# Loading q and k alike for both row groups, and the first stage's k and v in runs of tokens

## Chip, core and metric

The program runs on one core of one Trainium2 chip. The time is in device microseconds (us), and a kernel's figure is the median of its runs.

## What is computed

The input has 4 batches of 8 heads, 576 tokens and 64 numbers per head, all in fp32. The first half is attention with a rotary embedding, the second half a gated feed-forward block with a convolution over three tokens. The reference, cut to its core:

```python
def rotate(x):                      # x1, x2: the two halves of the 64 numbers of a token
    return concatenate([x1 * cos - x2 * sin, x1 * sin + x2 * cos])
scores = matmul(rotate(q), rotate(k).T) / sqrt(64)
attn = exp(scores - max(scores)) / sum
x = matmul(attn, v)                 # heads side by side: 4 x 576 x 512
h = maximum(x @ w_in, 0)            # 512 -> 1024
conv_out = sum of h[t - 1], h[t], h[t + 1], each times its row of conv_w
out = (h * sigmoid(conv_out)) @ w_out
```

## The kernel before, in words

**Pairs and steps.** Two heads make a pair, so there are 16 pairs, numbered p. A pair takes five steps (STEPS at L35): four blocks of 128 queries for each head, and a fifth with the last 64 queries of both. Pair p's first step is n = 5p. Nothing is left to a scheduler: `at(n, rank, fn)` (L695) puts a piece of work into step n, each step is written out in the order of its ranks, and each engine takes its instructions in that order. The DMA queue of SP is such an order too: an instruction of SP that has to wait holds up every later load on SP.

**Two stages.** Steps 0 to 25 (WIDE is 26, L681) are the first stage. In it the attention of pairs 0 to 4 runs beside the conversion of the fp64 weights to fp32 and to a high and a low part. From step 26 on, the matmuls of the feed-forward block fill the gaps of the attention.

**q and k.** A pair's q (or k) is loaded (`load`, L142 to L151) into a tile of 128 partitions. Each head has 64 of them, in two row groups of 32. Partition i of a group holds the 18 tokens 32c + i. The first group holds each token as it is (L149: one DMA of runs of 256 bytes), the second with its two halves exchanged (L150 and L151: two DMAs of runs of 128 bytes). So a part takes six DMAs. `rope` (L186) multiplies the tile on POOL with a table of the same layout, `tabt` (L190, six instructions), and adds the two halves (L193, three). That leaves x1 cos - x2 sin in the first group and x1 sin + x2 cos in the second. `emit_TQ` (L230) then transposes blocks of 32 x 32 on DVE into qT (L234) or kT (L237, all 18 blocks in one instruction); the last two k blocks go into the small tile kr as well (L241). The tiles rq and rk have one buffer each, so the next load waits for the transpose of the pair before. Pair 0 is loaded and rotated in another way (`load0`, `rope0`).

**Scores and softmax.** L261 and L287 make the scores of a block on PE, L269 its negated row maximum on DVE, L273 the exponentials on ACT, L321 and L352 turn them on PE, L199 copies them to `pt` on ACT.

**v.** `load_v` (L155) brings a pair's v at step n + 1: per head 512 tokens into the tile vm (L161, partition i holds the tokens i, 128 + i, ...) and the last 64 into vr (L162), four DMAs in all. `emit_E` (L383, the matmuls at L389) multiplies from step n + 5 on; head 0 and head 1 take turns over the four pieces of vm, and vr comes last.

**The sums.** `emit_rinv` (L363) takes the reciprocals of the row sums at step n + 5, writes them to DRAM in four small DMAs (L371) and reads them back spread over the partitions in three (L374 to L376, the tile rb). The norm (L403) multiplies with rb on DVE, at steps n + 8 and n + 9 in the first stage. Its high part is made on ACT (L406), the low part on POOL (L410).

**When loads are issued.** In the first stage q of pair p is loaded at step n - 9 and k at step n - 7, both with rank 19; the rope stands at step n - 6 with rank 18; the transposes of q stand at step n - 4, those of k at n - 2, with rank 0.45 (L723 to L726).

Of the kernel before, what the change touches and what calls it, by code (L numbers as in the profile page):

```python
# [20 lines left out]
def attention_moe_kernel(ctx, tc, q, k, v, w_in, conv_w, w_out, tab, tabx, out):  # L21
# [97 lines left out]

    raw = {}  # L120
    rot = {}

    def load0():
        r = raw[0] = {}
        for nm in ("q", "k"):
            r[nm] = wkeep.tile([128, 4, 2, D], F32, name="r" + nm)
        r["r"] = wkeep.tile([128, 2, D], F32, name="rr")

        def main(nm, src, eng):
            for h in range(2):  # L130
                eng.dma_start(out=r[nm][:, :, h, :], in_=src[0, h, 0:512, :].rearrange("(t p) d -> p t d", p=128))

        nc.sync.dma_start(out=tabs[:, 0:256], in_=tab[:, 0:256])
        main("q", q, nc.scalar)
        nc.sync.dma_start(out=tabs[:, 256:512], in_=tab[:, 256:512])
        main("k", k, nc.sync)
        nc.scalar.dma_start(out=tabs[:, 512:640], in_=tab[:, 512:640])
        nc.scalar.dma_start(out=idf, in_=tab[:, 640:768])
        nc.sync.dma_start(out=r["r"][0:64], in_=q[0, 0:2, 512:S, :].rearrange("h p d -> p h d"))
        nc.sync.dma_start(out=r["r"][64:128], in_=k[0, 0:2, 512:S, :].rearrange("h p d -> p h d"))  # L140

    def load(p, part):  # L142
        b, hp = divmod(p, NPB)
        x = raw[p, part] = p1.tile([128, S // 32, 2, 32], F32, tag="r" + part, name="r" + part)
        for h in range(2):
            y = (q if part == "q" else k)[b, 2 * hp + h].rearrange("(c i) d -> i c d", i=32)
            r0 = slice(64 * h, 64 * h + 32)
            r1 = slice(64 * h + 32, 64 * h + 64)
            nc.sync.dma_start(out=x[r0].rearrange("i c e d -> i c (e d)"), in_=y)  # L149
            nc.sync.dma_start(out=x[r1, :, 0, :], in_=y[:, :, 32:64])  # L150
            nc.sync.dma_start(out=x[r1, :, 1, :], in_=y[:, :, 0:32])  # L151

    vmain = {}

    def load_v(p):  # L155
        if p < 2:
            nc.vector.memset(vrem[p], 0.0)
        b, hp = divmod(p, NPB)
        t = vmain[p] = p1.tile([128, 2, 4, D], F32, tag="vm", name="vm", bufs=2)
        for h in range(2):  # L160
            nc.sync.dma_start(out=t[:, h], in_=v[b, 2 * hp + h, 0:512, :].rearrange("(t p) d -> p t d", p=128))  # L161
            nc.sync.dma_start(out=vrem[p % 2][64 * h:64 * h + 64, h, :], in_=v[b, 2 * hp + h, 512:S, :])  # L162

    def rope0(part, eng):
        x = raw[0][part]
# [19 lines left out]

    def rope(p, part):  # L186
        x = raw[p, part]
        for a in range(0, 18, 3):
            y = x[:, a:a + 3]
            nc.gpsimd.tensor_tensor(out=y, in0=y, in1=tabt[:, a:a + 3], op=ALU.mult)  # L190
        for a in range(0, 18, 6):
            y = x[:, a:a + 6]
            nc.gpsimd.tensor_tensor(out=y[:, :, 0, :], in0=y[:, :, 0, :], in1=y[:, :, 1, :], op=ALU.add)  # L193
# [36 lines left out]
    def emit_TQ(p, part):  # L230
        qk_tiles(p)
        x = raw.pop((p, part))[:, :, 0, :]
        if part == "q":
            nc.vector.transpose(out=QT[p].rearrange("p (c i) -> p c i", i=32), in_=x)  # L234
        else:
            kt = KT[p].rearrange("p (c i) -> p c i", i=32)
            nc.vector.transpose(out=kt[:, 2:20], in_=x)  # L237
            if p * STEPS < WIDE:
                for h in range(2):
                    r = slice(64 * h, 64 * h + 64)  # L240
                    nc.vector.transpose(out=krem[p % 2][r, r].rearrange("p (c i) -> p c i", i=32), in_=x[r, 16:18])  # L241
            if p * STEPS + STEPS > WIDE:
                nc.vector.transpose(out=kt[:, 0:2], in_=x[:, 16:18])
# [115 lines left out]
            at(late["n"], 5 if late["n"] > WIDE else 11, lambda dst=dst[:, i], ps=ps: evac("A", dst, ps))  # L359

    rb = {}

    def emit_rinv(p):  # L363
        rv = rvc[p % 2]
        rt = p1.tile([128, 32], F32, tag="rt", name="rt")
        nc.vector.tensor_scalar(out=rv[:, 0:9], in0=sums[p], scalar1=1e-9, scalar2=None, op0=ALU.add)
        nc.vector.reciprocal(out=rv[:, 0:9], in_=rv[:, 0:9])
        nc.vector.transpose(out=rt, in_=rv)
        d = scr.tile([9, 128], F32, tag="d", name="rd")
        for i in range(0, 128, 32):  # L370
            nc.sync.dma_start(out=d[:, i:i + 32], in_=rt[i:i + 9, :])  # L371
        fl = d.rearrange("(o t) n -> o (t n)", o=1)
        rbt = rb[p] = p1.tile([128, S], F32, tag="rb", name="rb")
        nc.sync.dma_start(out=rbt[0:64, :], in_=fl[:, 0:S].to_broadcast([64, S]))  # L374
        nc.sync.dma_start(out=rbt[64:128, 0:512], in_=fl[:, 640:1152].to_broadcast([64, 512]))
        nc.sync.dma_start(out=rbt[64:128, 512:S], in_=fl[:, 576:640].to_broadcast([64, 64]))  # L376
# [321 lines left out]
    def emit():  # L698
        with tc.manual_schedule(engines=engines):
# [5 lines left out]
            rope0("r", nc.vector)  # L705
            for part in "qrk":
                emit_TQ0(part)
            nc.sync.dma_start(out=tabt, in_=tabx.rearrange("p (c e d) -> p c e d", e=2, d=32))
            load(1, "q")
            load_w(0)  # L710
            emit_S(0, 0)
            load(1, "k")
            load_w(1)
            load_v(0)
# [3 lines left out]
            for p in range(1, NP):  # L718
                n = STEPS * p
                early = n - 10 >= WIDE - 1  # L720
                for i, part in enumerate("qk"):
                    if p > 1:
                        at(max(n - 10, WIDE) if early else n - 9 + 2 * i, 19.6 if early else 19, lambda p=p, part=part: load(p, part))  # L723
                    at(n - 8 + i if early else max(n - 6, 0), 18, lambda p=p, part=part: rope(p, part))
                    at(n - 5 + i * (n - 15 < WIDE) if early else max(n - 4 + 2 * i, 2), 0.45, lambda p=p, part=part: emit_TQ(p, part))
                at(n + 1, 19, lambda p=p: load_v(p))  # L726
            for p in range(NP):
# [19 lines left out]
                else:  # L747
                    for i in range(2):
                        m = n + 5 + (i if n + 5 < WIDE else 0)
                        at(m, 4 if m < WIDE else 10, lambda p=p, i=i: emit_E(p, i))  # L750
                at(n + 5, 4.5, lambda p=p: emit_rinv(p))
                for j in range(2):
                    at(n + NORM.get(p, 8 if n + 8 < WIDE else 7) + (j if p <= WIDE // STEPS else 0), 1.7 + j, lambda p=p, j=j: norms.pop((p, j))())
            whole, done = sum(c for c, _ in wsteps), 0
# [68 lines left out]
def _tables(S, D):  # L823
# [6 lines left out]
    for f in (np.cos(fr), np.sin(fr)):  # L830
# [5 lines left out]
    parts = [res[0], res[2], res[1], res[3], np.eye(128, dtype=np.float32)]  # L836
    root = float(D) ** -0.25
    cs = [(root * np.cos(fr)).astype(np.float32), (root * np.sin(fr)).astype(np.float32)]
    cs = [x.reshape(S // 32, 32, half).transpose(1, 0, 2) for x in cs]
    turned = [np.stack([cs[0], x], axis=2) for x in (-cs[1], cs[1])]  # L840
    return {
        "tab": np.ascontiguousarray(np.concatenate([x.reshape(128, -1) for x in parts], axis=1)),
        "tabx": np.ascontiguousarray(np.concatenate(turned * 2, axis=0).reshape(128, -1)),
    }


# [24 lines left out]
```

## Time and profile before

| what | value |
| --- | --- |
| runs | 482.95, 483.52 and 484.92 us; median 483.52 |
| profiled execution | span of 480.6 us from the first to the last instruction; its time with what lies around the span is not listed |
| PE, DVE, ACT, POOL busy | 450.5, 359.5, 331.9, 304.5 us |
| HBM read and written | 37.12 and 4.79 MB |

A row of the timeline gives the start and the duration in us, the engine, the line, what is written and read, and how many instructions are merged into the row; in brackets stands how long the engine had been idle and what ended that. "SPq" is SP's DMA queue: its rows are the issuing of a transfer, not the transfer.

### The profile page before, as it was taken

To read this page: it belongs to the slowest core of one execution; us is meant where nothing else is said; L and a number is where in the kernel's file an instruction comes from. 1 tells how busy PE (TensorE), PEld (TensorE's weight loads), DVE (VectorE), ACT (ScalarE), POOL (GpSimd) and SP (SyncE) were. 2 spreads that over 40 slices of the span, in tenths; PEclk is the share of its full clock that TensorE was granted. 3 is DMA by queue.
4 is the path that set the end of the run, shared out by engine and by line. 5 is a ranking of instruction groups with operands and counts; after the bars stand their busy time and mean duration, and the time that the engine had idled before them with its cause. 6 is when DMAs were issued, how large, how long until landed. Compare 5 with 4: busy or idle time off the path is not lost.

```text
span 480.6 us, 12404 instructions
## 1 busy us (share of the span) xinstructions
PE 450.5 (94%) x4572; PEld 355.8 (74%) x4572; DVE 359.5 (75%) x640; ACT 331.9 (69%) x951; POOL 304.5 (63%) x487
## 2 busy tenths in 40 slices
PE   1879887988999999999999999999999999999997
PEld 1446554656767787979788887879787978899886
DVE  5599899996898987777868686866874656467921
ACT  1699787887879786868778686867695953245510
POOL 3869999999797979393929394756530313144510
PEclk9999999899999999999999999999999999999999
DMA  9985877856436070718153362518020100100011
GB/s 186 245 138 158 175 179 143 152 117 161 74 81 142 9 149 25 137 37 134 39 99 74 78 95 60 103 40 145 9 66 16 49 13 25 46 22 23 0 67 44
DMA packets 140559, 42.71 MB, mean 89 GB/s; under 512 B 132156, under 2 KB 135252, under 8 KB 140500
## 3 DMA queue, kind: packets, MB, share of 16 engines
q1 hardware_dynamic: 139156, 41.54, 41.0%
q8 instruction: 36, 0.59, 0.5%
q10 hardware_dynamic: 1344, 0.39, 0.4%
q14 instruction: 23, 0.19, 0.1%
HBM read 37.12 MB, written 4.79 MB: 87 GB/s over the span
## 4 chain that ended last, share of the span: by engine, by line
PE 69%; DVE 9%; DMA 7%; SPq 7%; ACT 5%; issue 2%; POOL 0%; DVEq 0%; POOLq 0%
PE pm L431 13%; PE pm L540 11%; PE sp L261 11%; PE pm L389 11%; PE mt L520 10%; PE mt L431 7%; PE tp L321 5%; DVE negm L269 2%; DMA rd<-rt 2%; SPq L150 2%; DMA rq<-q 2%; ACT st L273 1%; ACT pt L199 1%; SPq L151 1%; DVE c L449 1%
## 5 line engine op out<-in xcount | busy, mean ns | idle before, releaser
L269 DVE TENSOR_REDUCE negm<-sp 128x1 f32<-128x576 f32 x144 | 102.5, 748 | 32.7 <-PE sp L261 24.1
L273 ACT ACTIVATE st<-sp,negm 128x576 f32<-128x576 f32 x128 | 93.7, 739 | 31.1 <-DVE negm L269 30.1
L261 PE MATMUL sp<-kT,qT 64*128 64x288 f32 (+4 forms) x556 | 98.7, 458 | 3.1 <-ACT st L273 1.3
L199 ACT ACTIVATE pt<-tp 128x512 f32<-128x512 f32 (+3 forms) x176 | 84.3, 532 | 3.7 <-PE tp L321 3.3
L449 DVE SCALAR_TENSOR_TENSOR c<-rr,cw,c 128x288 f32<-128x288 f32 x128 | 80.6, 629 | 4.2
L467 POOL TENSOR_TENSOR gm<-c,gm 128x288 fp32r<-128x288 f32 (+4 forms) x72 | 44.7, 626 | 49.7 <-ACT gm L466 49.7
L431 PE MATMUL pm<-xT,winh 128*128 128x290 f32 x352 | 74.5, 305 | 0.0
L190 POOL TENSOR_TENSOR rq<-rq,tabt 128x192 f32<-128x192 f32 x90 | 59.9, 698 | 11.7 <-DMA rq<-q 8.7
L410 POOL TENSOR_TENSOR xT<-xn,xT 128x290 fp32r<-128x290 f32 x32 | 29.5, 923 | 58.0 <-ACT xT L406 57.9
L261 PEld LDWEIGHTS sp<-kT,qT 64*128 64x128 f32 (+1 forms) x556 | 46.3, 176 | 24.2 <-issue 9.1
L321 PEld LDWEIGHTS tp<-idf,st 64*128 64x128 f32 x1024 | 42.6, 140 | 25.7 <-ACT st L273 12.9
L190 POOL TENSOR_TENSOR rk<-rk,tabt 128x192 f32<-128x192 f32 x90 | 56.9, 665 | 1.5 <-DMA rk<-k 1.1
L321 PE MATMUL tp<-idf,st 64*128 64x64 f32 x1024 | 49.4, 228 | 9.1 <-ACT st L273 7.3
L431 PEld LDWEIGHTS pm<-xT,winh 128*128 128x128 f32 x352 | 56.2, 189 | 1.8
L431 PE MATMUL pm<-xT,winl 128*128 128x290 f32 x176 | 52.0, 295 | 0.0
L389 PE MATMUL pm<-pt,vm 128*64 128x290 f32 x368 | 49.8, 411 | 0.4 <-ACT pt L199 0.4
L540 PE MATMUL pm<-wouth,gm 64*128 64x256 f32 x512 | 49.3, 281 | 0.0
L458 DVE SCALAR_TENSOR_TENSOR c<-c,rr 128x288 f32<-128x288 f32 x64 | 38.6, 624 | 10.4 <-ACT c L455 10.4
L540 PEld LDWEIGHTS pm<-wouth,gm 64*128 64x128 f32 x512 | 41.9, 185 | 0.0
L447 DVE TENSOR_SCALAR c<-rr,cw 128x288 f32<-128x288 f32 x56 | 24.9, 444 | 20.4 <-ACT rr L439 20.0
L389 PEld LDWEIGHTS pm<-pt,vm 128*64 128x64 f32 x368 | 25.6, 136 | 17.6 <-ACT pt L199 1.1
L540 PE MATMUL pm<-woutl,gm 64*128 64x256 f32 x256 | 37.7, 276 | 0.0
(118 smaller groups left out, 907.2 us busy)
## 6 DMA issues: line engine op xcount, KB each, us to landing
rq<-q SPq DMA_DIRECT2D x30, 144.0 KB
rq<-q SPq DMA_DIRECT2D x60, 72.0 KB
rk<-k SPq DMA_DIRECT2D x30, 144.0 KB
rk<-k SPq DMA_DIRECT2D x60, 72.0 KB
w<-moe_w_in SPq DMA_DIRECT2D x8, 512.0 KB
vm<-v SPq DMA_DIRECT2D x32, 128.0 KB
w<-moe_w_out SPq DMA_DIRECT2D x8, 512.0 KB
rb<-rd SPq DMA_DIRECT2D x16, 144.0 KB
```

The source lines that it names most:

```text
L190: nc.gpsimd.tensor_tensor(out=y, in0=y, in1=tabt[:, a:a + 3], op=ALU.mult)
L199: nc.scalar.activation(out=out, in_=in_, func=AF.Copy, scale=1.0 if sc is None else sc)
L261: nc.tensor.matmul(out=out, lhsT=qt[64 * h:64 * h + 64, c], rhs=kt[64 * h:64 * h + 64, a:a + n], start=True, stop=True)
L269: reds.setdefault((p, s), []).append(lambda: nc.vector.tensor_reduce(out=nm, in_=sc, axis=AX.XY if len(sc.shape) == 3 else AX.X, op=ALU.ma ...
L273: lambda: nc.scalar.activation(out=dst, in_=sc, func=AF.Exp, bias=nm, scale=1.0, accum_out=sm)
L321: nc.tensor.transpose(ps[r][:, 64 * k:64 * k + 64], x[i], idf[i, i])
L389: nc.tensor.matmul(out=xp[64 * h:64 * h + 64, :], lhsT=vmain[p][:, h, i, :] if i < 4 else vrem[p % 2][:, h, :], rhs=pt[:, 2 * i + h if i < ...
L431: nc.tensor.matmul(out=ps[:, 0:XW], lhsT=w[:, kk, fs], rhs=xT[:, xs, e, :], start=(i == 0), stop=(i == n - 1))
L449: nc.vector.scalar_tensor_tensor(out=c, in0=r[:, j + e:j + e + HS], scalar=cw[:, 8 * e + f:8 * e + f + 1], in1=c, op0=ALU.mult, op1=ALU.add,)
L467: nc.gpsimd.tensor_tensor(out=lo, in0=c[:, o:o + n], in1=hi.bitcast(F32), op=ALU.subtract)
L520: nc.tensor.matmul(out=ops[tt][:, 0:width], lhsT=g_tile(tt, f, e), rhs=w[:, f, cols], start=(f == 0 and i == 0), stop=(f == NF - 1 and i = ...
L540: nc.tensor.matmul(out=ps[r][:, 0:256], lhsT=g_tile(tt, f, e)[rows], rhs=w[rows, f, cols], start=(f == 0 and i == 0), stop=(f == NF - 1 an ...
```

## The change

All of q and k: both row groups of 32 are loaded alike, in four DMAs of runs of 256 bytes rather than six, and the second group's table has its sine and cosine exchanged in place of the halves. For pairs 1 to 6 (`runs(p)`) partition i of k holds the 18 tokens from 18i on, one run of 4,608 bytes; that needs a second table, `tabk`, which takes the place of pair 0's input tile (both have the tag "tk" in a pool with one buffer). The DVE transpose of such a k goes in two instructions, the first with its blocks in another order, so that 128 keys in a row of kT are those of four tokens of each partition. v of these pairs is loaded in the same order of keys, in 12 DMAs rather than four. The reading back of the sums (now `emit_rb`) is put a step later for pairs 0 to 3, at rank 17; the loads of q and k in the first stage get rank 16 rather than 19.

```diff
--- before.py
+++ after.py
@@ -119,12 +119,14 @@
 
     raw = {}
     rot = {}
+    tabk = {}
 
     def load0():
         r = raw[0] = {}
-        for nm in ("q", "k"):
-            r[nm] = wkeep.tile([128, 4, 2, D], F32, name="r" + nm)
-        r["r"] = wkeep.tile([128, 2, D], F32, name="rr")
+        x = wkeep.tile([128, 18 * D], F32, tag="tk", name="r0")
+        for i, nm in enumerate("qk"):
+            r[nm] = x[:, 512 * i:512 * i + 512].rearrange("p (t h d) -> p t h d", t=4, h=2)
+        r["r"] = x[:, 1024:1152].rearrange("p (h d) -> p h d", h=2)
 
         def main(nm, src, eng):
             for h in range(2):
@@ -143,14 +145,16 @@
         b, hp = divmod(p, NPB)
         x = raw[p, part] = p1.tile([128, S // 32, 2, 32], F32, tag="r" + part, name="r" + part)
         for h in range(2):
-            y = (q if part == "q" else k)[b, 2 * hp + h].rearrange("(c i) d -> i c d", i=32)
-            r0 = slice(64 * h, 64 * h + 32)
-            r1 = slice(64 * h + 32, 64 * h + 64)
-            nc.sync.dma_start(out=x[r0].rearrange("i c e d -> i c (e d)"), in_=y)
-            nc.sync.dma_start(out=x[r1, :, 0, :], in_=y[:, :, 32:64])
-            nc.sync.dma_start(out=x[r1, :, 1, :], in_=y[:, :, 0:32])
+            y = (q if part == "q" else k)[b, 2 * hp + h]
+            y = y.rearrange("(i c) d -> i c d", i=32) if part == "k" and runs(p) else y.rearrange("(c i) d -> i c d", i=32)
+            for g in range(2):
+                r = slice(64 * h + 32 * g, 64 * h + 32 * g + 32)
+                nc.sync.dma_start(out=x[r].rearrange("i c e d -> i c (e d)"), in_=y)
 
     vmain = {}
+
+    def runs(p):
+        return 0 < p and STEPS * p - 7 < WIDE - 2
 
     def load_v(p):
         if p < 2:
@@ -158,8 +162,16 @@
         b, hp = divmod(p, NPB)
         t = vmain[p] = p1.tile([128, 2, 4, D], F32, tag="vm", name="vm", bufs=2)
         for h in range(2):
-            nc.sync.dma_start(out=t[:, h], in_=v[b, 2 * hp + h, 0:512, :].rearrange("(t p) d -> p t d", p=128))
-            nc.sync.dma_start(out=vrem[p % 2][64 * h:64 * h + 64, h, :], in_=v[b, 2 * hp + h, 512:S, :])
+            if runs(p):
+                y = v[b, 2 * hp + h].rearrange("(i c) d -> i c d", i=32)
+                for c in range(4):
+                    nc.sync.dma_start(out=t[32 * c:32 * c + 32, h], in_=y[:, 4 * c:4 * c + 4])
+                for c in range(2):
+                    r = slice(64 * h + 32 * c, 64 * h + 32 * c + 32)
+                    nc.sync.dma_start(out=vrem[p % 2][r, h, :], in_=y[:, 16 + c])
+            else:
+                nc.sync.dma_start(out=t[:, h], in_=v[b, 2 * hp + h, 0:512, :].rearrange("(t p) d -> p t d", p=128))
+                nc.sync.dma_start(out=vrem[p % 2][64 * h:64 * h + 64, h, :], in_=v[b, 2 * hp + h, 512:S, :])
 
     def rope0(part, eng):
         x = raw[0][part]
@@ -185,9 +197,10 @@
 
     def rope(p, part):
         x = raw[p, part]
+        tb = tabk[0].rearrange("p (c e d) -> p c e d", e=2, d=32) if part == "k" and runs(p) else tabt
         for a in range(0, 18, 3):
             y = x[:, a:a + 3]
-            nc.gpsimd.tensor_tensor(out=y, in0=y, in1=tabt[:, a:a + 3], op=ALU.mult)
+            nc.gpsimd.tensor_tensor(out=y, in0=y, in1=tb[:, a:a + 3], op=ALU.mult)
         for a in range(0, 18, 6):
             y = x[:, a:a + 6]
             nc.gpsimd.tensor_tensor(out=y[:, :, 0, :], in0=y[:, :, 0, :], in1=y[:, :, 1, :], op=ALU.add)
@@ -234,7 +247,11 @@
             nc.vector.transpose(out=QT[p].rearrange("p (c i) -> p c i", i=32), in_=x)
         else:
             kt = KT[p].rearrange("p (c i) -> p c i", i=32)
-            nc.vector.transpose(out=kt[:, 2:20], in_=x)
+            if runs(p):
+                nc.vector.transpose(out=kt[:, 2:18].rearrange("p (t c) i -> p t c i", t=4), in_=x[:, 0:16].rearrange("p (c t) d -> p t c d", t=4))
+                nc.vector.transpose(out=kt[:, 18:20], in_=x[:, 16:18])
+            else:
+                nc.vector.transpose(out=kt[:, 2:20], in_=x)
             if p * STEPS < WIDE:
                 for h in range(2):
                     r = slice(64 * h, 64 * h + 64)
@@ -359,6 +376,7 @@
             at(late["n"], 5 if late["n"] > WIDE else 11, lambda dst=dst[:, i], ps=ps: evac("A", dst, ps))
 
     rb = {}
+    rds = {}
 
     def emit_rinv(p):
         rv = rvc[p % 2]
@@ -369,7 +387,10 @@
         d = scr.tile([9, 128], F32, tag="d", name="rd")
         for i in range(0, 128, 32):
             nc.sync.dma_start(out=d[:, i:i + 32], in_=rt[i:i + 9, :])
-        fl = d.rearrange("(o t) n -> o (t n)", o=1)
+        rds[p] = d
+
+    def emit_rb(p):
+        fl = rds.pop(p).rearrange("(o t) n -> o (t n)", o=1)
         rbt = rb[p] = p1.tile([128, S], F32, tag="rb", name="rb")
         nc.sync.dma_start(out=rbt[0:64, :], in_=fl[:, 0:S].to_broadcast([64, S]))
         nc.sync.dma_start(out=rbt[64:128, 0:512], in_=fl[:, 640:1152].to_broadcast([64, 512]))
@@ -705,10 +726,12 @@
             rope0("r", nc.vector)
             for part in "qrk":
                 emit_TQ0(part)
-            nc.sync.dma_start(out=tabt, in_=tabx.rearrange("p (c e d) -> p c e d", e=2, d=32))
+            nc.sync.dma_start(out=tabt, in_=tabx[0].rearrange("p (c e d) -> p c e d", e=2, d=32))
             load(1, "q")
             load_w(0)
             emit_S(0, 0)
+            tabk[0] = wkeep.tile([128, 18 * D], F32, tag="tk", name="tabk")
+            nc.sync.dma_start(out=tabk[0], in_=tabx[1])
             load(1, "k")
             load_w(1)
             load_v(0)
@@ -720,7 +743,7 @@
                 early = n - 10 >= WIDE - 1
                 for i, part in enumerate("qk"):
                     if p > 1:
-                        at(max(n - 10, WIDE) if early else n - 9 + 2 * i, 19.6 if early else 19, lambda p=p, part=part: load(p, part))
+                        at(max(n - 10, WIDE) if early else n - 9 + 2 * i, 19.6 if early else 16, lambda p=p, part=part: load(p, part))
                     at(n - 8 + i if early else max(n - 6, 0), 18, lambda p=p, part=part: rope(p, part))
                     at(n - 5 + i * (n - 15 < WIDE) if early else max(n - 4 + 2 * i, 2), 0.45, lambda p=p, part=part: emit_TQ(p, part))
                 at(n + 1, 19, lambda p=p: load_v(p))
@@ -749,6 +772,7 @@
                         m = n + 5 + (i if n + 5 < WIDE else 0)
                         at(m, 4 if m < WIDE else 10, lambda p=p, i=i: emit_E(p, i))
                 at(n + 5, 4.5, lambda p=p: emit_rinv(p))
+                at(n + 5 + (n + 8 < WIDE), 17 if n + 8 < WIDE else 4.6, lambda p=p: emit_rb(p))
                 for j in range(2):
                     at(n + NORM.get(p, 8 if n + 8 < WIDE else 7) + (j if p <= WIDE // STEPS else 0), 1.7 + j, lambda p=p, j=j: norms.pop((p, j))())
             whole, done = sum(c for c, _ in wsteps), 0
@@ -836,11 +860,13 @@
     parts = [res[0], res[2], res[1], res[3], np.eye(128, dtype=np.float32)]
     root = float(D) ** -0.25
     cs = [(root * np.cos(fr)).astype(np.float32), (root * np.sin(fr)).astype(np.float32)]
-    cs = [x.reshape(S // 32, 32, half).transpose(1, 0, 2) for x in cs]
-    turned = [np.stack([cs[0], x], axis=2) for x in (-cs[1], cs[1])]
+    orders = []
+    for a in ([x.reshape(S // 32, 32, half).transpose(1, 0, 2) for x in cs], [x.reshape(32, S // 32, half) for x in cs]):
+        turned = [np.stack([a[0], -a[1]], axis=2), np.stack([a[1], a[0]], axis=2)]
+        orders.append(np.concatenate(turned * 2, axis=0).reshape(128, -1))
     return {
         "tab": np.ascontiguousarray(np.concatenate([x.reshape(128, -1) for x in parts], axis=1)),
-        "tabx": np.ascontiguousarray(np.concatenate(turned * 2, axis=0).reshape(128, -1)),
+        "tabx": np.ascontiguousarray(np.stack(orders)),
     }
 
 
```

## Rows read from the trace of the kernel before

**Rows 1.** Windows by stage: busy us of each engine and instructions, PEclk, DMA share, GB/s.

```profile
20.00:110.00 90.00, 76.64 (x845) 48.18 (x843) 84.99 (x140) 77.55 (x205) 84.47 (x133) 0.98 0.74 159
110.00:180.00 70.00, 67.49 (x666) 51.75 (x662) 61.26 (x104) 59.79 (x172) 60.47 (x92) 1.00 0.48 98
180.00:380.00 200.00, 200.00 (x2388) 165.75 (x2386) 146.41 (x267) 151.95 (x446) 118.75 (x192) 1.00 0.36 72
```

**Rows 2.** Waits, 20 to 110 us: who waited for whom, us in total, times, longest.

```profile
POOL rq L190 <- DMA rq<-q: 2.8, 2, 2.6
...
DVE qT L234 <- POOL rq L193: 2.0, 3, 1.0
...
POOL rk L190 <- DMA rk<-k: 0.6, 1, 0.6
```

**Rows 3.** Timeline of POOL, pairs 2 and 3.

```profile
26.78 2.33 POOL L632 TENSOR_TENSOR winl<-wf,winh 128x128 fp32r<-128x128 f32 x4 [1.98 <-ACT winh L635]
31.71 4.42 POOL L190 TENSOR_TENSOR rq<-rq,tabt 128x192 f32<-128x192 f32 x6 [2.59 <-DMA rq<-q]
...
38.40 3.79 POOL L190 TENSOR_TENSOR rk<-rk,tabt 128x192 f32<-128x192 f32 x6 [0.63 <-DMA rk<-k]
...
50.96 0.80 POOL L410 TENSOR_TENSOR xT<-xn,xT 128x290 fp32r<-128x290 f32 x1
...
55.87 2.14 POOL L193 TENSOR_TENSOR rq<-rq 128x192 f32<-128x192 f32 x3
```

**Rows 4.** Timeline of DVE: start of the program, and the transposes of q and k.

```profile
10.92 0.21 DVE L184 TENSOR_TENSOR t1r<-t1r,rr 128x64 f32<-128x64 f32 x1
...
38.71 0.78 DVE L234 STREAM_TRANSPOSE qT<-rq 128x576 f32<-128x576 f32 x1 [0.19 <-issue]
...
58.05 0.78 DVE L234 STREAM_TRANSPOSE qT<-rq 128x576 f32<-128x576 f32 x1 [1.04 <-POOL rq L193]
...
106.25 0.77 DVE L237 STREAM_TRANSPOSE kT<-rk 128x576 f32<-128x576 f32 x1
...
107.42 0.24 DVE L243 STREAM_TRANSPOSE kT<-rk 128x64 f32<-128x64 f32 x1
```

**Rows 5.** Timeline of ACT.

```profile
24.61 0.75 ACT L273 ACTIVATE st<-sp,negm 128x576 f32<-128x576 f32 x1
...
48.83 0.45 ACT L406 ACTIVATE xT<-xn 128x290 fp32r<-128x290 f32 x1
```

**Rows 6.** Timeline of SP: issues of transfers.

```profile
10.46 0.43 SPq L149 DMA_DIRECT2D rk<-k  x1
...
25.80 0.34 SPq L149 DMA_DIRECT2D rq<-q  x1
...
28.86 0.50 SPq L151 DMA_DIRECT2D rq<-q  x1
...
36.14 1.38 SPq L371 DMA_DIRECT2D rd<-rt  x4
41.80 0.46 SPq L374 DMA_DIRECT2D rb<-rd  x1
...
43.59 0.59 SPq L161 DMA_DIRECT2D vm<-v  x1
...
45.41 0.51 SPq L162 DMA_DIRECT2D vr<-v  x1
```

**Rows 7.** Chain that ended last: start us, us, what (a transfer's piece runs to its landing).

```profile
43.59 2.44 DMA vm<-v
```

**Rows 8.** Timeline of PE.

```profile
24.79 0.46 PE L321 MATMUL tp<-idf,st 64*128 64x64 f32 x8 [0.45 <-ACT st L273]
...
50.49 1.21 PE L389 MATMUL sp<-pt,vm 128*64 128x145 f32 x16
51.52 0.42 PE L389 MATMUL sp<-pt,vr 128*64 128x145 f32 x4
```

**Rows 9.** DMA view, 46 to 50 us: GB/s in 40 equal slices.

```profile
GB/s 82 141 202 218 248 208 128 105 69 36 21 28 67 169 131 164 200 255 243 227 228 209 159 127 150 183 179 146 110 159 192 195 228 246 237 209 196 187 149 128
```

## The prediction

> **What bounds the kernel now.** I begin with the windows by stage [rows 1], because the change sits in the first stage. From 180 to 380 us PE is busy for all 200 us: there nothing that loads, ropes or transposes can move the end, unless it comes so late that PE stops. From 20 to 110 us no engine is full by itself, but DVE has 84.99 and POOL 84.47 of 90 us, PE only 76.64. DVE's instructions stand in one written order, and what it lacks to 90 us is 5 us. So from 20 to 110 us the time is DVE's work and its few gaps, and whatever shortens or lengthens that stretch moves the start of the PE-bound part, and the end with it.
>
> Next come the waits of that stretch [rows 2]. DVE waits three times for POOL's rope of q, 2.0 us in all; the largest case is 1.04 us at 58.05 [rows 4]. POOL in turn waits for q's loads for 2.8 us and for k's for 0.6. The timeline of POOL [rows 3] shows where: 2.59 us before 31.71 and 0.63 before 38.40, both for pair 2. After 38.40 POOL has practically no gap until 110 us. So the three waits of DVE hang on POOL's unbroken work, which began late because pair 2's load came late. That is what faster loads can reach: 2.0 us, and no more by this way.
>
> **Loads of q and k: a gain of 2.0 us.** For pair 2 the six issues of q run from 25.80 to 28.86 + 0.50 = 29.36 [rows 6], and POOL starts 2.35 us later, at 31.71. Four issues at the same pace (the six took 3.56 us, 0.59 each) end at 25.80 + 4 x 0.59 = 28.2, and there is a third less to move, in longer runs; I take POOL's start at 30.3, a lead of 1.4. k of pair 2 follows in four issues of long runs, so its 0.63 us should go too: lead 2.0 us. At 50.96 POOL's low part must wait for ACT's xT, which ends at 48.83 + 0.45 = 49.28 [rows 5]; POOL would be there at 48.96, so 0.3 is lost and 1.7 us of lead is left. The rope that ended at 55.87 + 2.14 = 58.01 then ends near 56.3, before DVE asks for it at 58.05 - 1.04 = 57.01. The other two waits together are 2.0 - 1.04 = 0.96 us; as DVE's own earlier time uses up the lead, 1.7 us has to cover 1.04 plus these 0.96 less what DVE spends more in between (next part, 1.0 by the end). It does. Gain 2.0; ends 0 (the lead is lost at a later wait) and 2.0.
>
> **The tables: nothing.** The rope keeps its shapes and its count, nine POOL instructions a part. The second table is 576 KB more, beside 576 KB for q and k each. Its load waits until pair 0's input is read for the last time, 10.92 + 0.21 = 11.13 [rows 4]. Queued behind it on SP are k of pair 1, three pieces of weights and v of pair 0. SP reached k at 10.46 [rows 6]; with two issues of q fewer (1.2 us) it reaches the table near 9.3, stands until 11.2 and issues k from about 11.8, 1.3 us later than before, but again with two issues fewer. Its cover if it is late: after pair 1's ropes POOL stands for 1.98 us before 26.78, waiting for ACT [rows 3]. So 0; ends -0.7 and +1.0, half of that cover.
>
> Pair 0's q, k and rest now share one tile. Were a wait set for a whole tile, DVE's first rope would wait for all loads. The trace excludes it: PE turns the first head's part of st at 24.79 [rows 8], while ACT writes the second head's part of that tile from 24.61 to 25.36 [rows 5].
>
> **DVE: a loss of 1.0 us.** k's transpose of 128x576 takes 0.77 us and one of 128x64 takes 0.24 [rows 4]. Two instructions of 512 and 64 columns cost about 0.77 x 512 / 576 + 0.24 = 0.92, that is 0.15 us more; I take 0.2, since the larger one also keeps its own start. Five of the six (pairs 1 to 5) lie before 110 us on the engine that sets the pace: 1.0 us. Ends: 0 if the pieces overlap, and 4.0 if the blocks in their other order run as four groups of 128 columns, at some 0.33 each by these two rows (0.8 more a pair). Pair 6's lies where PE is the bound: nothing.
>
> **v in 12 DMAs: a loss of 0.5 us.** Every issue costs SP about the same whatever it moves: the four of v take from 43.59 to 45.41 + 0.51 = 45.92, 0.58 each, the six of q 0.59. So v takes SP 12 x 0.58 = 7.0 us rather than 2.3. It also moves: q is now first, then rb, then v. For pair 1 (step 6): DVE's transpose of q ends at 38.71 + 0.78 = 39.49; q takes until 41.8; rb, 43.59 - 41.80 = 1.8, until 43.6; v until 50.6. A piece of v lands 2.44 us after its issue begins [rows 7]. The tenth of the twelve, the last of head 1's vm, begins at 43.6 + 9 x 0.58 = 48.8 and lands at 51.3; the last, vr, lands at 52.4. The product of pair 1 starts on PE at 50.49 and reaches vr at 51.52 [rows 8], so it would be 0.8 to 0.9 us late. PE has 13 us to spare in this stretch [rows 1], and DVE's next maxima wait only for what passes that slack: I take 0.5. For pairs 2 to 4 I take none. Ends 0 and 4.5 (all four pairs late, by about 1.1 each).
>
> Here a rule of the Trainium skill speaks against the change. What the trace shows first: q's and k's transfers are of 32 partitions each already, and where nothing else is under way they move some 200 to 250 GB/s [rows 9]; at 200, v's 288 KB need 1.5 us, far less than the 7.0 of their issues. The Trainium skill (SBUF — State Buffer, "Door 1: The DMA port swizzle") says that partitions 0 to 31 reach only 8 of 16 ports, and measures 189 GB/s there against 328 with all 128 partitions. By that, an estimate, v would need 0.7 us more and the sum would be 483.7 instead of 483.0.
>
> **Broadcasts of the sums: nothing.** SP no longer stands between rd (issued 36.14 to 37.52) and rb (41.80), 4.3 us for pair 0 [rows 6], so q is issued at once. rb(0) would go out at 41.8 to 43.6, as before, and the norm that needs it is two steps on. If it came late, DVE would stand before L403, the norm, with its maxima queued behind: ends 0 and +1.0.
>
> **The second stage: nothing.** Two issues fewer for each q and k; PE is full there [rows 1]. Pairs 5 and 6 still have v in 12 pieces, which delays pair 7's q by some 3 us on SP; POOL and DVE have room there, and PE covers it.
>
> **Sum.** -2.0 + 1.0 + 0.5 = -0.5 us. The profiled execution's span is 480.6 us; against it the sum is 480.1. The median of the runs is 483.52, 2.9 us above that span, which I carry over unchanged: **483.0 us**. A measurement of this kernel can tell about 0.5%, 2.4 us, from no change.
>
> **Rivals.** *v comes late in every pair (slower).* SP's queue is longer, and one issue in a full queue takes more; then the product at step n + 5 stands, PE's turns and the next scores stand behind it, and DVE's maxima behind those. It decides as soon as the tenth piece of v lands more than about 0.5 us after the product could start. For: pair 1's working above is already over that point. Against: PE's 13 us of idle time. At 1.1 us for four pairs, with 1.0 for DVE and nothing gained from POOL: 483.5 + 4.4 + 1.0 - 2.0 (if the gain holds) = 486.9, or 488.9 without it; I take 486.9.
>
> *All gains and no price (faster).* The transposes cost nothing more, v is in time, POOL's lead holds, and SP's earlier loads free another 1 us of DVE's 5 us of gaps: 483.5 - 3.0 = 480.5. For: DVE's gaps are there. Against: DVE's work itself, 85 of 90 us, is untouched.
>
> *The loads are faster and nothing wants it.* POOL gives its lead back at waits for ACT, DVE pays for its transposes: 483.5 + 1.0 + 0.5 = 485.0, still no change by the bound.
>
> **How the numbers follow.** The forecast 0.45, v late 0.2, all gains 0.25, nothing wanted 0.1. So faster 0.25, same 0.55, slower 0.2. The range goes from 480.0, the faster rival with a half us for the table, to 486.5, most of the slower one; it leaves out about 2 in 10.
>
> **What would show it.** Right: POOL's wait before pair 2's q rope about 1.2 us and none for k; no wait of DVE for POOL at q's transposes; two rows for k's transpose with about 0.95 us together; SP's issues in the order q, rb, v; the start of the PE-bound part half a us earlier. Wrong: PE waiting for vm or vr at L389 by more than 1 us a pair; DVE waiting for rb at L403; POOL waiting for the new table; a transpose over 1.2 us; or DVE's busy time from 20 to 110 us changed by more than 2 us, which none of these steps explains.

## The result, and the profile after

The changed kernel takes **486.7 us** (485.05 to 488.48, 10 runs), the kernel before 483.24 us beside it (481.96 to 485.54, 10 runs). The ratio is **1.0076 [1.0051, 1.0102]**: slower by 0.8%, more than the 0.5% that can be told from no change. The forecast was 483.0 us, its range ended at 486.5. The profiled execution took 485.71 us, with a span of 483.6 against 480.6.

The windows by stage of the kernel after, to be laid beside [rows 1]:

```profile
20.00:110.00 90.00, 76.28 (x839) 47.68 (x835) 84.50 (x145) 77.12 (x203) 84.80 (x133) 0.98 0.60 149
110.00:180.00 70.00, 66.88 (x633) 53.67 (x634) 58.03 (x101) 57.10 (x162) 57.04 (x89) 0.98 0.52 106
180.00:380.00 200.00, 200.00 (x2393) 165.20 (x2393) 145.98 (x266) 151.94 (x449) 120.41 (x194) 1.00 0.39 72
```

Look at the counts more than at the busy time. From 20 to 110 us PE does 839 matmuls instead of 845 and DVE is as busy as before. From 110 to 180 us PE does 633 instead of 666, DVE 58.0 us of work instead of 61.3, and PE's clock has fallen from 1.00 to 0.98. So the time is lost **after 110 us**, in a stretch that the prediction gave one paragraph. To see the place I numbered the 144 row maxima of DVE (L269 before, L286 after) from 0 in the two timelines and subtracted their starts: number 46, at 111 us, comes 0.24 us later than before; number 48 comes 5.8 us later, number 50 2.5, number 53 1.75, number 58 3.9 again, and from number 70 to the last it stays at 3.2 us.

The waits of the kernel after from 110 to 185 us name two suspects (who waited for whom, us in total, times, longest):

```profile
POOL rq L203 <- DMA rq<-q: 10.3, 3, 8.0
ACT st L290 <- DVE negm L286: 8.7, 5, 5.2
DVE rr L813 <- POOL rk L203: 7.3, 1, 7.3
```

Their places in the timeline of the kernel after, first DVE, POOL and ACT around the memset, then SP's queue and POOL's next rope:

```profile
112.94 0.21 DVE L386 STREAM_TRANSPOSE rt<-rvc 128x32 f32<-128x32 f32 x1
117.08 3.35 POOL L203 TENSOR_TENSOR rk<-rk,tabk 128x192 f32<-128x192 f32 x6 [0.62 <-DMA rk<-k]
...
120.50 0.06 DVE L813 MEMSET rr<- 128x2 f32 x1 [7.35 <-POOL rk L203]
...
121.28 0.74 ACT L290 ACTIVATE st<-sp,negm 128x576 f32<-128x576 f32 x1 [5.18 <-DVE negm L286]
...
113.50 1.89 SPq L389 DMA_DIRECT2D rd<-rt  x4
118.85 0.45 SPq L395 DMA_DIRECT2D rb<-rd  x1
...
121.75 1.87 SPq L168 DMA_DIRECT2D vm<-v  x4
...
126.50 0.83 SPq L171 DMA_DIRECT2D vr<-v  x2
127.43 1.98 SPq L152 DMA_DIRECT2D rq<-q  x4
...
132.85 4.00 POOL L203 TENSOR_TENSOR rq<-rq,tabt 128x192 f32<-128x192 f32 x6 [7.99 <-DMA rq<-q]
```

**A, the memset.** At step 26 the first stage's pool is closed and another pool takes its place. The first to write in that one is DVE, a memset of two columns of `rr` (L813). It now stands 7.35 us for POOL's rope of pair 6's k, the last reader of the new table `tabk`, which lies in the closed pool. Before, the same memset went through without a wait:

```profile
112.87 0.09 DVE L789 MEMSET rr<- 128x2 f32 x4
```

**D, q of pair 7.** SP issues it at 127.43, behind the twelve pieces of pair 5's v; before, it went out at 120.95. POOL starts its rope at 132.85 (before: 126.97), and DVE needs what follows from it. The rows of the kernel before:

```profile
115.64 0.46 SPq L374 DMA_DIRECT2D rb<-rd  x1
...
117.47 0.54 SPq L161 DMA_DIRECT2D vm<-v  x1
...
120.95 0.58 SPq L149 DMA_DIRECT2D rq<-q  x1
...
126.97 4.28 POOL L190 TENSOR_TENSOR rq<-rq,tabt 128x192 f32<-128x192 f32 x6 [2.94 <-DVE negm L269]
```

(The bracket of the last row names a row maximum of DVE, which this rope does not read.)

### The profile page after: what moved, and what is told of

Read it like the earlier page. It is cut to its first block, busy times and chain, and to the rows that moved or that the text cites. A ratio compares the mean times of both kernels' runs of the same rounds, so it can differ in the third digit from the quotient of the medians.

```text
span 483.6 us, 12405 instructions
## 1 busy us (share of the span) xinstructions
PE 452.7 (94%) x4572; PEld 359.4 (74%) x4572; DVE 357.5 (74%) x646; ACT 331.9 (69%) x951; POOL 304.7 (63%) x487
## 2 busy tenths in 40 slices
DMA packets 88287, 43.30 MB, mean 90 GB/s; under 512 B 77452, under 2 KB 82084, under 8 KB 88228
## 4 chain that ended last, share of the span: by engine, by line
PE 70%; POOL 13%; DMA 5%; DVE 5%; ACT 3%; SPq 2%; issue 2%; POOLq 0%; DVEq 0%
PE pm L452 13%; PE sp L278 12%; PE pm L561 11%; PE pm L410 11%; PE mt L541 10%; PE mt L452 7%; PE tp L338 5%; POOL rk L203 3%; POOL rq L203 3%; DMA rk<-k 2%; DMA rq<-q 2%; POOL rq L206 2%; POOL winl L653 2%; DVE negm L286 1%; POOL woutl L653 1%
## 5 line engine op out<-in xcount | busy, mean ns | idle before, releaser
L286 DVE TENSOR_REDUCE negm<-sp 128x1 f32<-128x576 f32 x144 | 102.5, 748 | 28.6 <-PE sp L278 20.1
L278 PE MATMUL sp<-kT,qT 64*128 64x288 f32 (+4 forms) x556 | 99.8, 461 | 3.4 <-ACT st L290 1.7
L488 POOL TENSOR_TENSOR gm<-c,gm 128x288 fp32r<-128x288 f32 (+4 forms) x72 | 45.8, 641 | 48.3 <-ACT gm L487 48.3
L431 POOL TENSOR_TENSOR xT<-xn,xT 128x290 fp32r<-128x290 f32 x32 | 28.5, 892 | 58.7 <-ACT xT L427 58.7
L410 PE MATMUL pm<-pt,vm 128*64 128x290 f32 x368 | 50.2, 411 | 0.2 <-ACT pt L212 0.2
L410 PEld LDWEIGHTS pm<-pt,vm 128*64 128x64 f32 x368 | 27.7, 136 | 15.3 <-ACT pt L212 0.6
L468 DVE TENSOR_SCALAR c<-rr,cw 128x288 f32<-128x288 f32 x56 | 23.6, 422 | 19.9 <-ACT rr L460 19.5
L476 ACT ACTIVATE c<-c 128x288 f32<-128x288 f32 x64 | 28.5, 445 | 10.0 <-DVE c L470 10.0
```

The lines of the kernel that those rows point to most:

```text
L278: nc.tensor.matmul(out=out, lhsT=qt[64 * h:64 * h + 64, c], rhs=kt[64 * h:64 * h + 64, a:a + n], start=True, stop=True)
L286: reds.setdefault((p, s), []).append(lambda: nc.vector.tensor_reduce(out=nm, in_=sc, axis=AX.XY if len(sc.shape) == 3 else AX.X, op=ALU.ma ...
L410: nc.tensor.matmul(out=xp[64 * h:64 * h + 64, :], lhsT=vmain[p][:, h, i, :] if i < 4 else vrem[p % 2][:, h, :], rhs=pt[:, 2 * i + h if i < ...
L488: nc.gpsimd.tensor_tensor(out=lo, in0=c[:, o:o + n], in1=hi.bitcast(F32), op=ALU.subtract)
```

## Experiments

Each row is a median with its range, and the ratio to runs of the kernel before beside it.

| run | edit | time, us | ratio |
| --- | --- | --- | --- |
| e1_tilewait | after, no memset wait | 486.13 (485.25 to 487.71, 10 runs) | 1.006 [1.003, 1.0089] |
| e2_runs5 | after, k and v of pair 6 as before | 486.27 (485.83 to 486.81, 8) | 1.0059 [1.0033, 1.0085] |
| e9_q7first | after, q of pair 7 ahead of v | 486.4 (484.84 to 488.56, 12) | 1.0052 [1.0023, 1.0081] |
| e5_qfirst | after, both | 482.57 (481.75 to 484.29, 12) | 0.9979 [0.9953, 1.0005] |
| e4_holdb | before, with a memset wait | 487.05 (486.22 to 487.42, 6) | 1.0076 [1.0049, 1.0104] |
| e6_cutv56 | before, v of pairs 5 and 6 in 12 DMAs | 486.32 (484.6 to 488.78, 12) | 1.0058 [1.003, 1.0086] |
| e7_alikeonly | only q and k loaded alike | 482.12 (481.11 to 485.81, 12) | 0.997 [0.994, 1.0] |
| e3_noruns | e7, with the broadcasts moved | 482.04 (480.76 to 485.63, 12) | 0.9972 [0.9942, 1.0001] |
| e8_q2early | e3, q of pair 2 loaded at the start | 481.64 (480.28 to 484.57, 12) | 0.9957 [0.9928, 0.9987] |

**e1_tilewait: the changed kernel without the memset's wait.** The new pools wait tile by tile for what lay in their place, and the tiles of pair 0's rotation are allocated first, so that `rr` does not come to lie on `tabk`.

```diff
+        for part, n in (("q", 8), ("k", 8), ("r", 2)):
+            rot[part] = wkeep.tile([128, n, D], F32, name="t1" + part)
...
-                    rpool = ctx.enter_context(tc.tile_pool(name="rpool", bufs=1))
+                    rpool = ctx.enter_context(tc.tile_pool(name="rpool", bufs=1, reuse_waits="tile"))
...
```

> The change whole, but the pools opened at step 26 wait tile by tile for what lay there before, and the first stage's pool is laid out so that the new tiles rr do not lie where the second table lies. Theory A (DVE's clearing of rr waits for POOL's last rope that reads the second table): the 7.35 us before the clearing of rr fall to under 0.3, the next maxima start near 115 us instead of 120.5, and the time is that of the kernel before to 1 us, about 483.5. Rival B (v in 12 pieces comes late and PE stalls): no change, 486 to 487. Rival C (a second stretch at half clock near 111 us costs it): 485 to 487, with that stretch still in the profile.

486.13 us: the wait is gone and the time is still there. The timeline of this kernel shows what stands behind the memset once it is out of the way:

```profile
113.42 0.09 DVE L815 MEMSET rr<- 128x2 f32 x4
...
127.98 2.00 SPq L154 DMA_DIRECT2D rq<-q  x4
...
133.50 4.43 POOL L205 TENSOR_TENSOR rq<-rq,tabt 128x192 f32<-128x192 f32 x6 [8.10 <-DVE c L481]
...
147.56 0.78 DVE L256 STREAM_TRANSPOSE kT<-rk 128x576 f32<-128x576 f32 x1 [3.25 <-POOL rk L208]
...
151.19 1.71 PE L280 MATMUL sp<-kT,qT 64*128 64x288 f32 x7 [2.86 <-ACT st L292]
```

q of pair 7 is issued at 127.98, POOL stands 8.10 us before its rope (the row names DVE's work on c, which ends at that moment but is not read by this rope; the load's issue ends 3.5 us earlier, as it does in the kernel after, whose row names the load), k's rope follows late, DVE waits 3.25 us to transpose it, and PE stands 2.86 us for the scores. In the changed kernel the same transpose waits only 0.48 us, since the memset had already made DVE late:

```profile
147.06 0.78 DVE L254 STREAM_TRANSPOSE kT<-rk 128x576 f32<-128x576 f32 x1 [0.48 <-POOL rk L206]
```

**e2_runs5: another way to shorten the table's life.** Pair 6 keeps the old order, so `tabk` is read for the last time by pair 5.

```diff
-        return 0 < p and STEPS * p - 7 < WIDE - 2
+        return 0 < p < 6
```

> The change, but pair 6 is taken out of the runs, so that the last reader of the second table is pair 5's rope, near 105 us. Theory A: no wait before the clearing of rr, about 483.5 us. Rival B: five of six pairs still have v in 12 pieces, so 486 or a little less. Rival C: 485 to 487.

486.27 us. There is no wait at the memset (113.60), and the same 3.25 us at k's transpose:

```profile
146.76 0.78 DVE L254 STREAM_TRANSPOSE kT<-rk 128x576 f32<-128x576 f32 x1 [3.25 <-POOL rk L206]
```

Two different edits that take away A bring back 0.6 and 0.4 us at most.

**e3_noruns: neither the second table nor the cut v.** q and k are loaded alike, the broadcasts are moved.

```diff
-        return 0 < p and STEPS * p - 7 < WIDE - 2
+        return False
...
-            tabk[0] = wkeep.tile([128, 18 * D], F32, tag="tk", name="tabk")
-            nc.sync.dma_start(out=tabk[0], in_=tabx[1])
...
```

> Only q and k loaded alike with the swapped table, and the broadcasts a step later behind q; no runs, no second table, v as before in four DMAs. Theory A and rival B: both 483 us, 0 to 1 us below the kernel before. By the terms of the prediction: no second transpose (saves 1.0 us against the change) and v in time (0.5), so DVE's waits for POOL under 1 us if the loads give POOL its lead; if POOL's wait for pair 2's q is as long as with the change (3.4 us), the loads gain nothing and the time is 483.2 to 484.

482.04 us, a little below what any theory expected: all of the loss sits in the runs of tokens and what they bring with them, the table and the pieces of v.

**e4_holdb: A by itself, in the kernel before.** POOL touches an old table in the first stage's pool after it has roped pair 6's k.

```diff
+        if (p, part) == (6, "k"):
+            nc.gpsimd.memset(tabs[:, 0:8], 0.0)
```

> The kernel before, with one tiny POOL instruction behind pair 6's rope of k that writes 8 columns of a tile of the first stage's pool (0.1 us of work). Theory A: DVE's clearing of rr waits from about 113 to 121.7 us and the time rises by 2 to 4 us, to about 486. Rivals B and C: no change, 483.2.

487.05 us, as slow as the whole change. Its timeline:

```profile
121.28 0.06 DVE L791 MEMSET rr<- 128x2 f32 x1 [8.40 <-POOL tabs L195]
...
122.95 2.10 PE L263 MATMUL sp<-kT,qT 64*128 64x288 f32 x7 [3.05 <-ACT st L275]
```

A single instruction of 0.12 us on POOL, in the wrong place, costs 3.9 us, because it keeps DVE from its row maxima for 8.40 us and PE from its scores for 3.05.

**e5_qfirst: both taken away.** e1 with pair 7's q issued ahead of pair 5's v.

```diff
-  ... 19.6 if early else 16, lambda p=p, part=part: load(p, part))
+  ... (18.9 if (p, part) == (7, "q") else 19.6) if early else 16, lambda p=p, part=part: load(p, part))
```

> The run with tile-by-tile waits, and pair 7's q loaded ahead of pair 5's v at step 26 instead of behind it. Theory D (once the wait for the table is gone, the next thing late is pair 7: its q stands on SP behind 12 pieces of v, POOL's rope of it starts at 133.5 instead of 127.0 us, and DVE's transpose of its k waits 3.25 us at 147.6): POOL's rope of pair 7's q starts before 130 us, that transpose waits under 0.6 us, and the time falls from 486.1 to 483 to 484.5. Rival E (the runs cost it elsewhere, by DVE's further transposes or v's late landing): 486.

482.57 us, no slower than before and a little under the 483 to 484.5 expected. The timeline shows q issued at the old time and no wait at k's transpose:

```profile
120.73 1.96 SPq L154 DMA_DIRECT2D rq<-q  x4
...
126.26 4.10 POOL L205 TENSOR_TENSOR rq<-rq,tabt 128x192 f32<-128x192 f32 x6 [1.94 <-DMA rq<-q]
...
143.43 0.76 DVE L256 STREAM_TRANSPOSE kT<-rk 128x576 f32<-128x576 f32 x1
```

**e6_cutv56: D by itself, in the kernel before.** The same v, in the old order, in 12 DMAs for pairs 5 and 6.

```diff
-            nc.sync.dma_start(out=t[:, h], in_=v[b, 2 * hp + h, 0:512, :].rearrange("(t p) d -> p t d", p=128))
+            y = v[b, 2 * hp + h]
+            for c in range(0, 128, 32 if 4 < p < 7 else 128):
+                r = slice(c, c + (32 if 4 < p < 7 else 128))
+                nc.sync.dma_start(out=t[r, h], in_=y[0:512].rearrange("(t p) d -> p t d", p=128)[r])
...
```

> The kernel before, with v of pairs 5 and 6 alone loaded in 12 DMAs instead of four; the same data in the same places, nothing else changed. Theory D: pair 7's q is issued some 3.3 us later, POOL's rope of it starts near 130.3 instead of 127.0, its k is ready near 145.5 and DVE waits about 2 us for it at 143.2: 484.5 to 485.5. Rival E: no change, 483.2.

486.32 us, more than the 484.5 to 485.5 expected. The profiled execution was 1.45 us late already at the memset (114.32 against 112.87), where nothing is edited; from there its timeline has e1's pattern:

```profile
126.38 0.37 SPq L149 DMA_DIRECT2D rq<-q  x1
...
132.32 4.36 POOL L195 TENSOR_TENSOR rq<-rq,tabt 128x192 f32<-128x192 f32 x6 [6.42 <-DMA rq<-q]
...
146.53 0.78 DVE L242 STREAM_TRANSPOSE kT<-rk 128x576 f32<-128x576 f32 x1 [2.13 <-POOL rk L198]
...
150.17 1.71 PE L266 MATMUL sp<-kT,qT 64*128 64x288 f32 x7 [1.90 <-ACT st L278]
```

The early 1.45 us are not the cost: at row maximum 53 (131 us) 0.22 us of lateness are left, and from number 58 on, behind the transpose that waits, it is 3.1 to 3.7 us.

**e7_alikeonly: the loads alone**, with rb and the order of loads as before. Against e3:

```diff
-  ... 19.6 if early else 16, lambda p=p, part=part: load(p, part))
+  ... 19.6 if early else 19, lambda p=p, part=part: load(p, part))
...
-                at(n + 5 + (n + 8 < WIDE), 17 if n + 8 < WIDE else 4.6, lambda p=p: emit_rb(p))
+                at(n + 5, 4.6, lambda p=p: emit_rb(p))
```

> Only q and k loaded alike with the swapped table; the broadcasts and the order of loads as in the kernel before. If the loads' shape is what made the run without runs 482.0 us: 482 again. If it was the broadcasts' place: 483.2, as before. POOL's wait before pair 2's q rope stays 2.6 to 3.4 us in either case, since four issues took as long to land as six.

482.12 us, beside e3's 482.04: the moved broadcasts are worth nothing. The ratio, 0.997, has 1.0 at the end of its interval, and the profiled execution shows no cause for a gain: POOL still waits 3.2 us for pair 2's q, DVE 3.1 us for POOL's ropes of q, and the last row maximum comes 0.04 us later than before. Whether the loads gain up to 0.6% or nothing stays open.

**e8_q2early: what an early q of pair 2 would have brought.** e3, with this q loaded into pair 0's tile at the start of the program.

```diff
+        if (p, part) == (2, "q"):
+            x = raw[p, part] = wkeep.tile([128, 18 * D], F32, tag="tk", name="r2").rearrange("p (c e d) -> p c e d", e=2, d=32)
...
+            load(2, "q")
...
```

> The run without runs, and pair 2's q loaded at step 0 into the place of pair 0's input tile, so that POOL need not wait for it. If the three waits of DVE for POOL come from POOL's late start of pair 2 (as the prediction had it): POOL's 3.3 us before pair 2's q rope are gone, DVE's waits for POOL's q ropes fall from 2.5 to under 0.8 us and the time falls by 1 to 2 us, to about 480.5. If POOL gives the lead back at its wait for ACT's xT near 49 us and at DVE's weights: no change, 482.

481.64 us, 0.4% less than before: faster by its interval, though within the 0.5%. The waits of its first stage:

```profile
POOL winl L656 <- ACT winh L659: 5.7, 1, 5.7
...
POOL xT L434 <- ACT xT L430: 1.7, 1, 1.7
...
DVE qT L250 <- POOL rq L209: 1.0, 1, 1.0
```

POOL's wait for this q is gone, and POOL waits for ACT instead, 5.7 us (3.2 in e3, 1.98 before [rows 3]) and 1.7. DVE's waits for POOL's q ropes fall to 1.0 us (2.5 in e3, 2.0 before). Yet in the profiled executions the last row maximum comes only 0.26 us earlier than before, and 0.6 us later than in e3. So the lead that the prediction wanted is mostly given back, as its third rival had it.

**e9_q7first: D taken away, A left.** The changed kernel with e5's rank alone.

> The changed kernel with one difference: pair 7's q is issued ahead of pair 5's v in step 26; the second table keeps its place in the first stage's pool. With this the four cases of the two causes are complete. Theory: each cause alone is enough, since the second one only finds what slack the first has left. The memset of rr waits some 7.3 us for POOL's last rope with the second table, as in the changed kernel; k's transpose of pair 7 then has no wait of over 0.5 us; and the time stays at 486.0 to 487.2, ratio about 1.0065, because DVE's slack was already spent at the memset. Rival 1 (the late q is the cause and the memset is only a symptom of it): 482.6, as with both removed. Rival 2 (the costs add, half each): some 484.5.

486.4 us. The timeline:

```profile
121.30 0.06 DVE L813 MEMSET rr<- 128x2 f32 x1 [8.10 <-POOL rk L203]
...
122.98 2.53 PE L278 MATMUL sp<-kT,qT 64*128 64x288 f32 x7 [2.01 <-ACT st L290]
...
124.82 1.98 SPq L152 DMA_DIRECT2D rq<-q  x4
...
146.89 0.77 DVE L254 STREAM_TRANSPOSE kT<-rk 128x576 f32<-128x576 f32 x1
```

Pair 7's q is ahead of v here, but its tile is free only after DVE's late transpose of pair 6's q (123.67 + 0.77), so it goes out 3.9 us later than before; k's transpose waits for nothing all the same.

That completes the square: with both causes 486.7, with D alone 486.13 and 486.27, with A alone 486.4, with neither 482.57. **The two do not add**; each alone costs nearly all. What A makes late, D has no need to make late again. In the changed kernel's own profile both can be seen: the 5.8 us of row maximum 48 have shrunk to 1.75 at number 53, and number 58, behind k's transpose, is 3.9 us late. So taking away one at a time, the usual way to look for a cause, clears both of them, and only e5, and the two placed by themselves into the kernel before, show them.

**Where PE loses it.** For each kernel I took PE's idle time from 110 to 180 us (70 less its busy time) and added 1.7 us for each stretch at a low clock, in which the windows show 0.83 over 10 us, 0.17 x 10 = 1.7 us of full clock. In windows of 2 us such a stretch falls to 0.50, the lower of the clock's two levels, 1.2 GHz.

| kernel | PE idle, us | low-clock stretches | sum | span |
| --- | --- | --- | --- | --- |
| before | 2.51 | none | 2.5 | 480.6 |
| e3 / e7 / e8 | 1.74 / 2.67 / 2.56 | none | 1.7 / 2.7 / 2.6 | 479.5 / 480.4 / 480.1 |
| e5 | 2.53 | none | 2.5 | 480.0 |
| after | 3.12 | 110 to 116 us | 4.8 | 483.6 |
| e9 | 3.84 | 122 to 128 | 5.5 | 484.0 |
| e6 | 4.11 | 152 to 156 | 5.8 | 483.7 |
| e4 | 4.28 | 124 to 128 | 6.0 | 484.1 |
| e2 | 4.69 | 152 to 156 | 6.4 | 483.7 |
| e1 | 4.24 | 112 to 116, 152 to 156 | 7.6 | 484.5 |

The rows of one window, 120 to 130 us, in the kernel before and then in e4:

```profile
120.00:130.00 10.00, 9.09 (x99) 7.33 (x101) 8.74 (x12) 8.15 (x25) 7.06 (x13) 1.00 0.41 74
```

```profile
120.00:130.00 10.00, 7.05 (x54) 5.77 (x56) 7.27 (x15) 7.48 (x22) 3.61 (x9) 0.83 0.45 89
```

99 matmuls against 54, in the same 10 us: PE stands for 3.05 us, and then runs part of what follows at half its clock. The sums order the spans roughly, and the five kernels with neither A nor D are the five with the small sums. Single runs of the kernel before have low-clock stretches too: of its 35 runs beside e6, the seven with a mean granted clock of 1.0 took 482.3 us on the mean, the seven at 0.989 486.0. That alone is not the difference between the kernels: at 0.995 to 0.996, three runs of e6 took 485.5 us on the mean and thirteen of the kernel before 482.7. In the kernel after itself the low clock comes first, from 110 us on, before DVE's wait has reached PE; the same stretch stands in e1 and not in e9, e2 and e5, with the same short stops of PE ahead of it (1.04 and 0.52 us; 1.05 and 0.52 in e9). So it is no part of A or D, and what brings it stays open.

## Why the prediction was wrong, step by step

**The second stage: nothing.** This step failed. Its words: pairs 5 and 6 still have v in 12 pieces, "which delays pair 7's q by some 3 us on SP; POOL and DVE have room there, and PE covers it." The delay was 6.5 us (127.43 against 120.95). In the kernel after v begins 4.3 us later, 121.75 against 117.47, behind the read-back of the sums, which waits until 118.85 instead of 115.64; its pieces then take 5.6 us instead of 3.4. Why the read-back is late was not tried by itself; in the five profiles with runs of tokens it waits 3.5 to 4.0 us after the sums are issued, in the six without 1.3 to 2.3, and in the five two loads of weights of 512 KB stand within 4 us ahead of the sums on SP, in the six one. The pieces alone are enough: in e6 q goes out 4.0 us later than its early 1.45 us explain, and that run loses as much. And PE covers only a part. In e4 DVE's maxima are 6.6 us late at the memset and 3.8 us at number 50, since the kernel before has a wait of DVE for PE of 3.19 us in between, at 121.15; of these 3.8 us, 3.5 are left at the end. That PE is full for the 200 us from 180 on [rows 1] means that what it loses before is not made up there. From 110 to 180 us it is fed step by step by DVE's maxima, and there it has 2.5 us of idle time, not a store of work.

**The tables: nothing.** This step failed too. It asked when the second table arrives (POOL waited 0.79 us for k of pair 1, 0.49 before, and never for the table) and not how long it has to stay. Pair 6's rope, the last to read it, stands after the point at which the pool's place is given on; e4 prices that at 3.9 us by itself.

**Loads of q and k: 2.0 us of gain.** This gain did not come. Four issues end at 28.76 instead of 29.36, where 28.2 was foreseen. Nor is there "a third less to move": six DMAs of a q carried 2 x 144 + 4 x 72 = 576 KB, four carry 4 x 144 = 576. The issues by size, before and then after:

```profile
rq<-q SPq DMA_DIRECT2D x30, 144.0 KB
rq<-q SPq DMA_DIRECT2D x60, 72.0 KB
```

```profile
rq<-q SPq DMA_DIRECT2D x60, 144.0 KB
```

And the data came later, not earlier. The chain that ended last in the kernel after, and its POOL timeline, beside [rows 3]:

```profile
27.34 4.95 DMA rq<-q
```

```profile
32.40 4.42 POOL L203 TENSOR_TENSOR rq<-rq,tabt 128x192 f32<-128x192 f32 x6 [3.45 <-DMA rq<-q]
...
38.61 4.50 POOL L203 TENSOR_TENSOR rk<-rk,tabk 128x192 f32<-128x192 f32 x6
```

The last piece needs 4.95 us from issue to landing, and POOL starts at 32.40 where I had 30.3 and where it had been 31.71. Only k's 0.63 us went, in e7 too, where k has no runs of tokens. DVE's waits for POOL's ropes of q grew from 2.0 to 2.5 us.

**DVE: a loss of 1.0 us.** The mechanism was right and the size too large. The transpose in two instructions of the kernel after, and what follows them:

```profile
106.48 0.70 DVE L251 STREAM_TRANSPOSE kT<-rk 128x512 f32<-128x512 f32 x1
107.11 0.20 DVE L252 STREAM_TRANSPOSE kT<-rk 128x64 f32<-128x64 f32 x1
107.23 0.45 DVE L258 STREAM_TRANSPOSE kr<-rk 64x64 f32<-64x64 f32 x2
```

From the first to the next work are 0.75 us; before it was 106.94 - 106.25 = 0.69. So a pair costs 0.06 us more, 0.3 for five, and the blocks in their other order cost nothing.

**v in 12 DMAs: 0.5 us, and the rival "v comes late in every pair".** PE never waits for v at L410 in the first stage; pair 1's product starts at 50.55 (before: 50.49). The 12 issues take 44.34 to 50.03, 0.47 us each rather than 0.58, and the last of them ends before that product starts; so the 0.5 us does not show. The pieces do harm by what stands behind them on SP, a place where neither the step nor the rival looked. The rival's sum, 486.9, is close to the result by chance.

**Broadcasts: nothing.** Right (e3 against e7). DVE's wait for rb in the first stage is 0.3 us, once.

The whole first stage, for which I had 0.5 us of gain, ends 0.24 us later. That this is near is luck: 2.0 us of gain and 1.5 of loss were both too large and nearly cancelled. The error is the 3 us after it. Of the signs that the prediction named, SP's order, k's missing wait and the two rows of k's transpose (0.70 and 0.20 us) came as foreseen; POOL's short wait for q, DVE without waits for POOL, and an earlier start of the PE-bound part (it comes 3.2 us later) did not. Of the signs of being wrong none came: PE did not wait for vm or vr, nor DVE for rb by more than 0.3 us, nor POOL for the new table, and no transpose took over 1.2 us. All of these lay before 110 us, and none would have shown what happened.

## What to carry to other kernels

Of a new tile ask not only when it is filled but when it is last read, and who is the first to write where its pool lay: here that instruction waited, with everything queued behind it, until in e1 the new pools waited tile by tile and the tile lay elsewhere. A full engine downstream is no promise of cover: a delay is hidden only as far as the upstream engine had been waiting anyway, and what PE loses beyond that stays lost. And where undoing one suspect brings nothing back, put each suspect by itself into the kernel before, and undo two together, before either is cleared.

## What was not expected of the hardware

- **A stall of PE cost more than itself.** In e4 and e9 PE stands 3.05 and 2.01 us at 122.9; in e6, e2 and e1 1.90, 2.85 and 2.86 us at 150 to 151. In all five a stretch at the lower clock begins within about 2 us of PE's return and is worth 1.7 us of full clock. In e5, where PE stands for 0.28 us at most there, and for 1.09 us at 128.1, none follows.
- **A low clock where there is slack cost nothing.** The kernel before has such a stretch at 84 to 88 us, and e7 has none. Against the kernel before, e7's row maxima come 0.54 us late at 83 us, 0.28 us early at 91 us and 0.55 us late again at 100 us: the 0.8 us that it gains are gone.
- **Fewer packets did not bring this q sooner.** The same bytes of q went in four DMAs rather than six, and the program's packets fell from 140,559 to 88,287, those under 512 B from 132,156 to 77,452. Yet POOL started on pair 2's q 0.7 us later than before, after a wait of 3.45 us (2.59 before, 3.2 in e7).
